# Head-mixing attention, routed experts and a dense layer in one kernel: scores and weighted sums move behind the transposing product of a slot

## The chip, the cores and the metric

The kernel runs on one core of one Trainium2 chip. The metric is the device time of one execution in microseconds (us), taken as the median of the runs shown. Engines are named as in the profile: PE is TensorE (PEld its weight loads), DVE is VectorE, ACT is ScalarE, POOL is GpSimd, SP is the engine whose queue starts most of the DMA transfers.

## The reference, cut to what matters

Three layers follow one another. The change touches the first one, attention with two mixes over the heads (4 batches, 12 heads, 448 positions, 64 values per head, all float32):

```python
scores = scale * np.matmul(q, k.transpose(0, 1, 3, 2))
scores = np.einsum('bhij,hg->bgij', scores, w_pre)
scores = scores - np.max(scores, axis=-1, keepdims=True)
attn = np.exp(scores)
attn = attn / (np.sum(attn, axis=-1, keepdims=True) + 1e-09)
attn = np.einsum('bhij,hg->bgij', attn, w_post)
return np.matmul(attn, v).astype(np.float32)
```

Its output feeds a layer of 8 routed experts, and that one a dense layer `g = h - tanh(h)` between two matrix products.

## The kernel before, in words

**Tiles and blocks.** The 4 x 448 query rows are cut into 16 tiles T of 120, 120, 120 and 88 rows per batch. A tile is cut into blocks of 10 rows (the last of a batch into 8 of 10 and one of 8), 180 blocks in all. A block holds 10 rows x 12 heads = 120 partitions, so that a mix over the heads is one product with a 120 x 120 matrix.

**The slot loop (L1013 to L1045).** One slot is one turn of a loop over s, written out in the order in which each engine is to do its work; there is no other planner. Each engine works through its own instructions in that order, and waits where a buffer or an input is not there yet. In slot s the kernel issues:

- P(s) (`emit_P`, L363): the head mix of block s on PE, as 2 matmuls into a PSUM bank of tag "b" (2 buffers). DVE takes the row maximum `mx` (L371); ACT makes p = exp (L374) and its sum.
- `emit_W` (L378) of block s-1 on DVE: the reciprocal of that sum and `w` = the second mixing matrix scaled by it (L381, L382, L384). It stands behind `mx` of block s on DVE.
- T(s-2) (`emit_T`, `T_mm`, L390 to L407): the transposing product of block s-2 on PE, 8 matmuls that mix the heads again, divide by the sum and turn the block, into a bank of tag "c" (2 buffers). It reads p and w of block s-2. ACT copies it out into A (`emit_TE`, L411).
- Fills, at slots fixed by formulas (`posS2`, `posAV`, `at_e`, L860 to L923): `emit_S2` (L428) makes the scores of 4 heads, 12 matmuls (L324), the first pair of heads into the two banks of tag "a", the second pair into "d" and "e" (one buffer each); ACT copies out the first pair (`ssb`, L331), then the bank "d" (`ssb`, L328), DVE the bank "e" (`ssb`, L329). `emit_AV2` (L438, L424) makes the weighted sums of 4 heads of a finished tile, 32 matmuls into bank "d", copied out by ACT (`xT`, L426). `tr_q` and `tr_k` transpose inputs into bank "e", copied out by ACT (`qh` L304, `kh` L287) and DVE (`ql` L305, `kl` L288). `emit_X` (L449) uses "e" as well.
- Routing pieces (`emit_R`, L483): small products R and M that each take one of the two "c" banks, and DVE work on them.
- Converting a piece of a later layer's weights (`conv_do`, L111): three DVE instructions (`ct`, L115 to L117), three on POOL (`cm`, L118 to L120).

Copies out of `emit_S`/`emit_S2` are issued at once; those of the other fills are kept in a list and issued by `flush` at the start of the next slot, or earlier when their bank is wanted again (`flush("d")`, `flush("e")`). DMA: `relay_to` (L939) sends a block's rows of the scores to `sr`, 8 buffers, 7 slots ahead of the P that reads them.

**Which slots have what.** Counted from the formulas, 44 of the 180 slots have a scores fill and 44 a weighted-sums fill; six (35, 42, 80, 87, 125 and 132) have both, so 38 have scores alone and 38 weighted sums alone. In a slot with both, scores come first. R stands in slots 64, 109, 154 and 177, M two slots later. Slot 180 has weighted sums and T(178), and no P.

The order in a slot is set by these lines:

```python
            ex = emit_P(s) if s < NBK else lambda: None
            if 0 <= s - 1 < NBK:
                emit_W(s - 1)
            ...
            fill.sort(key=lambda x: x[0] not in (emit_S, emit_S2, emit_AV2))
            if fill and fill[0][0] in (emit_S, emit_S2, emit_AV2):
                run_fill(*fill.pop(0))
            ex()
            ...
            if on:
                emit_T(i)
                T_mm(i, 0, NJ)
                flush("d")
                emit_TE(i)
            for x in fill:
                run_fill(*x)
```

`ex()` issues the exp of the slot; behind it stands the DVE and POOL work of `conv_do`. So PE's order in a slot with one such fill is P, fill, T, and the exp stands behind the copies of the scores on ACT. In a slot with both it is P, scores, T, weighted sums.

Of the kernel before, what the change touches and what calls it, by code (L numbers as in the profile page):

```python
# [30 lines left out]
def body(ctx: ExitStack, tc, q, k, v, w_pre, w_post, emb, tau, w1, w2, win, wout, out):  # L31
# [93 lines left out]
    if True:  # L125
# [237 lines left out]
        def emit_P(i):  # L363
            n = 12 * blocks[i][2]
            t = sr.pop(i)
            pt = ps("b", f"P{i}")
            pe.matmul(pt[:n, :S], wpre[:n, :n], t[:n, :], start=True, stop=True)  # L367

            flush2()
            mx = a2.tile([120, 4], F32, tag="mx", name=f"mx{i}", bufs=5)  # L370
            dve.tensor_reduce(mx[:n, 0:1], pt[:n, :S], op=ALU.max, axis=AX.X, negate=True)  # L371
            p = a2.tile([120, S], F32, tag="p", name=f"p{i}", bufs=LAG + 1)
            pj[i] = (p, mx)
            return lambda: act.activation(p[:n, :], pt[:n, :S], AF.Exp, bias=mx[:n, 0:1], scale=1.0, accum_out=mx[:n, 1:2])  # L374
# [3 lines left out]
        def emit_W(i):  # L378
            n = 12 * blocks[i][2]
            p, mx = pj[i]  # L380
            dve.tensor_scalar_add(mx[:n, 2:3], mx[:n, 1:2], 1e-9)  # L381
            dve.reciprocal(mx[:n, 3:4], mx[:n, 2:3])  # L382
            w = a2.tile([120, 120], F32, tag="w", name=f"w{i}", bufs=3)
            dve.tensor_scalar_mul(w[:n, :], wpost[:n, :], mx[:n, 3:4])  # L384
            wj[i] = w
# [4 lines left out]
        def emit_T(i):  # L390
            T, r, m = blocks[i]
            n = 12 * m
            b, it = divmod(T, 4)
            if r == 0:
                A[T] = aA.tile([CP, NJ, H, 120], F32, tag="A", name=f"A{T}", bufs=2)
            p, mx = pj.pop(i)
            w = wj.pop(i)
            wv = w.rearrange("p (g i) -> p g i", i=10)[:n, :, :m]
            pt = ps("c", f"T{i}")
            pv = pt[:CP, :NJ * n].rearrange("p (c g i) -> p c g i", c=NJ, i=m)  # L400
            tev[i] = (pt, pv, p, w, wv, n, m)

        def T_mm(i, c0, c1):
            pt, pv, p, w, wv, n, m = tev[i]
            for c in range(c0, c1):
                pe.matmul(pt[:CP, c * n:(c + 1) * n] if m == 10 else pv[:, c], p[:n, c * CP:(c + 1) * CP], w[:n, :] if m == 10 else wv,  # L406
                          start=True, stop=True)  # L407

        def emit_TE(i):
            T, r, m = blocks[i]  # L410
            act.copy(A[T][:, :, :, 10 * r:10 * r + m], tev.pop(i)[1])  # L411
# [202 lines left out]
    with mctx:  # L614
# [324 lines left out]
        def relay_to(i):  # L939
            while nxt[0] <= min(i, NBK - 1) and blocks[nxt[0]][0] in sdone:  # L940
                emit_relay(nxt[0])
                nxt[0] += 1
# [4 lines left out]
        def flush(tag=None):  # L947
            keep = []
            while late:
                x = late.pop(0)  # L950
                if tag in (None, x[0]):
                    y = x[1]()
                    if x[0] == "e" and callable(y):
                        late2.append((x[0], y))
                else:
                    keep.append(x)
            late.extend(keep)
            if tag:
                flush2(tag)
# [9 lines left out]
        def run_fill(fn, a):  # L969
            tag = "d" if fn is emit_AV2 else "e"  # L970
            if fn is emit_S2:
                flush("d")
                flush("e")
            elif fn is not emit_S:
                flush(tag)
            e = fn(*a)
            if fn in (emit_S, emit_S2):
                e()
                if a[1] + (fn is emit_S2) == NP - 1:
                    sdone.add(a[0])  # L980
            else:
                late.append((tag, e))
# [30 lines left out]
        for s in range(NBK + LAG + 6):  # L1013
            todo = side.get(s, [])
            fill = [x for x in todo if x[0] in PEF]
            for fn, a in todo:
                if fn in (load_q, load_k, load_v, conv_load, zero_fill):
                    fn(*a)
            flush()
            relay_to(s + NSR - 1)  # L1020
# [3 lines that stand above are left out]
            for fn, a in todo:  # L1024
                if fn is emit_R and a[1] in (0, 1, 3):
                    fn(*a)
            i = s - LAG
            on = 0 <= i < NBK
            fill.sort(key=lambda x: x[0] not in (emit_S, emit_S2, emit_AV2))
            if fill and fill[0][0] in (emit_S, emit_S2, emit_AV2):  # L1030
                run_fill(*fill.pop(0))
            ex()
            for fn, a in todo:
                if fn is conv_do:
                    fn(*a)
# [7 lines that stand above are left out]
            for fn, a in todo:  # L1043
                if fn in (to_experts, do1) or fn is emit_R and a[1] in (2, 4):
                    fn(*a)  # L1045
# [334 lines left out]
```

## Time and profile before

| | before |
|---|---|
| median of 3 runs | 1370.86 us (1370.37 to 1372.72) |
| the profiled execution | 1376.32 us, its span 1374.6 us |
| mean granted clock of PE | 0.977 of full speed |
| PE busy | 1312.8 us, 96% of the span |
| DVE busy | 1017.7 us, 74% |
| ACT busy | 736.7 us, 54% |
| POOL busy | 502.8 us, 37% |

The slot loop fills the span from about 24 us to 516 us; the experts and the dense layer follow. Busy times are unions per engine; a matmul's own duration overlaps its neighbour's, so that start-to-start distances tell what one costs PE.

### The profile page before, as it was taken

How to read it: one execution, taken by the hardware profiler on the slowest of the kernel's cores; microseconds unless marked ns; L12 is line 12 of the kernel's file. 1: busy time of each engine (PE TensorE's matmuls, PEld its weight loads, DVE VectorE, ACT ScalarE, POOL GpSimd, SP SyncE). 2: the span in 40 equal slices, each digit the busy share in tenths (PEclk: the TensorE clock that was granted, in tenths of full speed). 3: DMA queues.
4: the chain of work that ended last, by engine and by line, in shares of the span. 5: the costliest groups of instructions: out<-in, count | busy, mean ns of one | idle time of the engine just before them, and what ended most of it. 6: DMA issues, size and time to landing. Idle time of an engine off the chain costs nothing. (4 is left out here: it accounts for less than half of the span.)

```text
span 1374.6 us, 24956 instructions
## 1 busy us (share of the span) xinstructions
PE 1312.8 (96%) x9104; PEld 1146.0 (83%) x9104; DVE 1017.7 (74%) x2189; ACT 736.7 (54%) x1518; POOL 502.8 (37%) x495
## 2 busy tenths in 40 slices
PE   7999999999999987999999997899999989999998
PEld 5777776776777766999999996699998889999998
DVE  4776787678677773677776764688888788788886
ACT  5666666675666653545444453554444444544441
POOL 0233333333333323333332422544454334444432
PEclk9999999999999997999999999799999999999999
DMA  6886675667556564778877872421113133121102
GB/s 153 247 253 190 185 209 168 170 201 202 160 173 204 164 205 147 263 253 262 273 233 238 254 220 84 136 69 47 46 48 109 37 96 107 67 61 55 47 24 81
DMA packets 149412, 210.90 MB, mean 153 GB/s; under 512 B 54022, under 2 KB 109494, under 8 KB 149286
## 3 DMA queue, kind: packets, MB, share of 16 engines
q1 hardware_dynamic: 145104, 194.19, 46.4%
q0 software_dynamic: 2640, 12.19, 2.8%
q10 hardware_dynamic: 1542, 2.89, 0.7%
q8 instruction: 73, 1.20, 0.4%
q14 instruction: 53, 0.43, 0.1%
HBM read 135.70 MB, written 35.00 MB: 124 GB/s over the span
## 5 line engine op out<-in xcount | busy, mean ns | idle before, releaser
L406 PEld LDWEIGHTS T<-w,p 120*112 120x112 f32 (+1 forms) x1440 | 166.4, 177 | 66.8 <-issue 44.5
L120 POOL TENSOR_TENSOR cm<-cm,ct 128x256 f32<-128x256 f32 x96 | 70.1, 731 | 404.9 <-DVE ct L117 360.9
L406 PE MATMUL T<-w,p 120*112 120x120 f32 (+1 forms) x1440 | 185.6, 272 | 6.2 <-DVE w L384 3.0
L374 ACT ACTIVATE p<-P,mx 120x448 f32<-120x448 f32 x180 | 114.0, 633 | 119.8 <-DVE mx L381 106.3
L1220 POOL TENSOR_TENSOR gl<-th,gh 128x448 fp32r<-128x448 f32 x64 | 74.8, 1169 | 261.0 <-ACT gh L1219 192.6
L367 PE MATMUL P<-sr,wpre 120*120 120x448 f32 x360 | 166.2, 544 | 1.4 <-ACT p L374 1.4
L1271 PE MATMUL o<-woh,gh 128*128 128x384 f32 x448 | 152.5, 340 | 5.3 <-DVE acc L1277 5.3
L1240 ACT ACTIVATE u<-h 128x448 f32<-128x448 f32 x64 | 34.9, 546 | 222.9 <-PE h L1236 219.2
L1272 PE MATMUL o<-wol,gh 128*128 128x384 f32 x448 | 150.7, 336 | 0.0
L1273 PE MATMUL o<-woh,gl 128*128 128x384 f32 x448 | 150.7, 336 | 0.0
L371 DVE TENSOR_REDUCE mx<-P 120x1 f32<-120x448 f32 x180 | 111.4, 619 | 49.4 <-PE P L367 48.6
L1236 PE MATMUL h<-yh,wil 128*128 128x448 f32 x384 | 143.8, 374 | 3.3 <-POOL wil L1209 3.3
L1234 PE MATMUL h<-yh,wih 128*128 128x448 f32 x384 | 144.0, 375 | 1.1 <-ACT wih L1208 0.6
L1277 DVE TENSOR_TENSOR acc<-acc,o 128x384 f32<-128x384 f32 x196 | 106.9, 548 | 51.4 <-PE o L1273 51.4
L1235 PE MATMUL h<-yl,wih 128*128 128x448 f32 x384 | 143.9, 375 | 0.5 <-DVE yl L1183 0.5
L411 ACT COPY A<-T 112x480 f32<-112x480 f32 x180 | 101.5, 564 | 16.2 <-PE T L406 15.6
L686 PE MATMUL hi<-xhi,w1hi 128*128 128x256 f32 x384 | 108.8, 283 | 0.0
L687 PE MATMUL hi<-xli,w1hi 128*128 128x256 f32 x384 | 108.6, 283 | 0.0
L688 PE MATMUL hi<-xhi,w1li 128*128 128x256 f32 x384 | 108.4, 282 | 0.0
L424 PEld LDWEIGHTS AV<-A,v 112*64 112x64 f32 x1536 | 74.8, 138 | 23.9 <-issue 10.5
L669 PE MATMUL ypi<-w2hi,hhi 128*128 128x384 f32 x272 | 93.2, 343 | 0.1
L670 PE MATMUL ypi<-w2li,hhi 128*128 128x384 f32 x272 | 92.1, 338 | 0.6 <-DVE w2li L639 0.3
(223 smaller groups left out, 3279.9 us busy)
## 6 DMA issues: line engine op xcount, KB each, us to landing
sr<-ssb SPq DMA_DIRECT2D x176, 210.0 KB
r<-in_moe_w SPq DMA_DIRECT2D x72, 384.0 KB
r<-in_moe_w SPq DMA_DIRECT2D x52, 512.0 KB
craw<-in_moe_w_in SPq DMA_DIRECT2D x48, 256.0 KB
craw<-in_moe_w_out SPq DMA_DIRECT2D x48, 256.0 KB
raw<-wi_d SPq DMA_DIRECT2D x15, 768.0 KB
wor<-wo_d SPq DMA_DIRECT2D x15, 768.0 KB
wi_d<-cm SPq DMA_DIRECT2D x48, 128.0 KB
```

The costliest lines, as they stand in the source:

```text
L367: pe.matmul(pt[:n, :S], wpre[:n, :n], t[:n, :], start=True, stop=True)
L371: dve.tensor_reduce(mx[:n, 0:1], pt[:n, :S], op=ALU.max, axis=AX.X, negate=True)
L374: return lambda: act.activation(p[:n, :], pt[:n, :S], AF.Exp, bias=mx[:n, 0:1], scale=1.0, accum_out=mx[:n, 1:2])
L406: pe.matmul(pt[:CP, c * n:(c + 1) * n] if m == 10 else pv[:, c], p[:n, c * CP:(c + 1) * CP], w[:n, :] if m == 10 else wv, start=True, stop ...
L686: pe.matmul(pt[:, :256], wh[:, sl], xh[:, c, :], start=c == 0, stop=False)
L687: pe.matmul(pt[:, :256], wh[:, sl], xl[:, c, :], start=False, stop=False)
L1234: pe.matmul(pt[:, :S], wi[0][:, c, sl], yh[:, c, :], start=c == 0, stop=False)
L1235: pe.matmul(pt[:, :S], wi[0][:, c, sl], yl[:, c, :], start=False, stop=False)
L1236: pe.matmul(pt[:, :S], wi[1][:, c, sl], yh[:, c, :], start=False, stop=c == KD - 1)
L1271: pe.matmul(pt[:, :384], gh[:, sl], wo[0][:, f, n0:n0 + 384], start=f == 0, stop=False)
L1272: pe.matmul(pt[:, :384], gh[:, sl], wo[1][:, f, n0:n0 + 384], start=False, stop=False)
L1273: pe.matmul(pt[:, :384], gl[:, sl], wo[0][:, f, n0:n0 + 384], start=False, stop=f == GF - 1)
```

## The change

The two lines that run the first scores or weighted-sums fill ahead of `ex()` are gone. The fill stays in the list, at its head, and is run by the loop behind `emit_TE`. In a slot with one such fill PE's order becomes P, T, fill; in a slot with both it becomes P, T, scores, weighted sums. On ACT the exp and the copy of T come ahead of the copies of the scores; on DVE `conv_do` comes ahead of the copy of bank "e". No instruction is added or taken away.

```diff
             i = s - LAG
             on = 0 <= i < NBK
             fill.sort(key=lambda x: x[0] not in (emit_S, emit_S2, emit_AV2))
-            if fill and fill[0][0] in (emit_S, emit_S2, emit_AV2):
-                run_fill(*fill.pop(0))
             ex()
             for fn, a in todo:
                 if fn is conv_do:
```

## Rows read from the trace of the kernel before

**Rows 1.** Busy time by engine in the slot loop; columns: stretch, us, PE, PEld, DVE, ACT, POOL, clock, DMA.

```profile
24.00:510.00 486.00, 477.04 (x4092) 352.54 (x4092) 357.53 (x1114) 322.21 (x769) 160.71 (x219) 1.00 0.67 197
```

**Rows 2.** PE in order of time, slot 71, no such fill; columns: start, us, instruction.

```profile
211.28 0.92 PE L367 MATMUL P<-sr,wpre 120*120 120x448 f32 x2
212.03 0.98 PE L406 MATMUL T<-w,p 120*112 120x120 f32 x8
212.85 0.55 PE L281 MATMUL ptk<-ident,natk 112*128 112x112 f32 x4
```

**Rows 3.** PE in order of time, slot 42, which has both fills, and the next P.

```profile
132.26 0.46 PE L324 MATMUL S<-kh,qh 64*120 64x448 f32 x2
...
133.67 1.07 PE L406 MATMUL T<-w,p 120*112 120x120 f32 x8
134.72 1.86 PE L424 MATMUL AV<-A,v 112*64 112x120 f32 x32
136.51 1.01 PE L367 MATMUL P<-sr,wpre 120*120 120x448 f32 x2
```

**Rows 4.** DVE in order of time, slots 41 and 42: mx(41), w(40), mx(42).

```profile
131.60 0.61 DVE L371 TENSOR_REDUCE mx<-P 120x1 f32<-120x448 f32 x1
...
132.50 0.28 DVE L384 TENSOR_SCALAR w<-wpost,mx 120x120 f32<-120x120 f32 x1
132.70 0.62 DVE L371 TENSOR_REDUCE mx<-P 120x1 f32<-120x448 f32 x1
```

**Rows 5.** ACT in order of time, slots 41 and 42: copy of T, copies of the scores.

```profile
132.87 0.56 ACT L411 COPY A<-T 112x480 f32<-112x480 f32 x1
133.31 0.92 ACT L331 ACTIVATE ssb<-S 120x896 f32<-120x896 f32 x1
134.12 0.55 ACT L328 ACTIVATE ssb<-S 120x448 f32<-120x448 f32 x1
```

**Rows 6.** PE in order of time, slot 35: the scores' second pair of heads, the next P.

```profile
112.32 0.46 PE L324 MATMUL S<-kh,qh 64*120 64x448 f32 x1 [0.53 <-DVE kl L288]
...
115.90 1.01 PE L367 MATMUL P<-sr,wpre 120*120 120x448 f32 x2
```

**Rows 7.** DVE in order of time, slot 35: mx(35).

```profile
112.18 0.61 DVE L371 TENSOR_REDUCE mx<-P 120x1 f32<-120x448 f32 x1
```

**Rows 8.** All engines in order of time, slot 132: mx(132), and the next P.

```profile
387.77 0.62 DVE L371 TENSOR_REDUCE mx<-P 120x1 f32<-120x448 f32 x1
...
390.46 0.64 PE L367 MATMUL P<-sr,wpre 120*120 120x448 f32 x1
```

**Rows 9.** All engines in order of time, slots 9 and 174: P(s), w(s-2).

```profile
41.71 0.92 PE L367 MATMUL P<-sr,wpre 120*120 120x448 f32 x2
42.85 0.28 DVE L384 TENSOR_SCALAR w<-wpost,mx 120x120 f32<-120x120 f32 x1
...
494.05 0.92 PE L367 MATMUL P<-sr,wpre 120*120 120x448 f32 x2
494.87 0.28 DVE L384 TENSOR_SCALAR w<-wpost,mx 120x120 f32<-120x120 f32 x1
```

**Rows 10.** All engines in order of time, slots 64 and 154, which have R: weighted sums, A.

```profile
191.09 1.86 PE L424 MATMUL AV<-A,v 112*64 112x120 f32 x32
191.36 0.56 ACT L411 COPY A<-T 112x480 f32<-112x480 f32 x1
...
445.03 1.86 PE L424 MATMUL AV<-A,v 112*64 112x120 f32 x32
445.76 0.56 ACT L411 COPY A<-T 112x480 f32<-112x480 f32 x1
```

**Rows 11.** All engines in order of time, slot 180: weighted sums, w(178).

```profile
512.86 2.88 PE L424 MATMUL AV<-A,v 112*64 112x120 f32 x32
513.16 1.69 DVE L384 TENSOR_SCALAR w<-wpost,mx 120x120 f32<-120x120 f32 x1
```

**Rows 12.** Busy time by engine and granted clock, last slots of the loop; columns as in rows 1.

```profile
510.00:515.00 5.00, 3.12 (x36) 3.03 (x38) 4.86 (x9) 2.22 (x6) 4.01 (x2) 0.85 0.44 130
```

## The prediction

> **What bounds the kernel now.** I read the busy time of the stretch that the change touches first, then PE's order of time in three kinds of slot, and then DVE's and ACT's beside it. In the 486 us of the slot loop PE is busy for 477.04 us, at the full granted clock; DVE and ACT have 357.53 and 322.21 us [rows 1]. So PE sets the pace, 2.7 us a slot, with 9 us of pauses in all. The same matmuls run after the change, so PE's work stays; what can change is how long PE waits, and PE's next wait is what to look for. A slot without these fills costs PE 0.75 us for P (211.28 to 212.03) and 0.82 us for T [rows 2]. Scores take 1.41 us and weighted sums 1.79 us [rows 3]. Today these 1.4 or 1.8 us stand between P and T, and so they are a reserve: whatever T needs may come that much later than P's end and costs nothing. After the change the reserve is gone, and the fill has it: whatever the fill needs may come 0.8 us later than now.
>
> **The change part by part.** All terms are against the profiled execution (1376.32 us, which is 5.5 us over the median of the runs shown); I carry their sum over to the median.
>
> *A, slots with both fills (six).* Now T stands between scores and weighted sums on PE; after the change nothing does, and both use the one bank "d". The weighted sums can begin only when ACT has copied the scores out of it (`ssb`, L328), and that copy now stands behind the exp, the copy A of T and the other score copy. ACT's chain from the maximum on: mx starts at 131.60, A at 132.87, that is 1.27 us [rows 4, 5]; A to the first score copy 0.44 us, first to second copy 0.81 us, the second lasts 0.55 us [rows 5]; together 3.07 us from the start of mx(s) to a free bank. In slot 42 mx(42) starts at 132.70 [rows 4], so the bank is free at 135.77, the weighted sums end 1.79 us later at 137.56, and P follows there, now at 136.51 [rows 3]: 1.05 us lost. (T(40) waits for w(40), which ends at 132.78 [rows 4], half a microsecond after it could begin; this wait lies inside the 1.05.) Slot 87 shows the same times. In slot 35 mx starts at 112.18 [rows 7], the bank is free at 115.25, P follows at 117.04 instead of 115.90 [rows 6]: 1.14 us, and slots 80 and 125 repeat it. In slot 132 mx starts late, at 387.77: 390.84, then 392.63 instead of 390.46 [rows 8], 2.17 us. Sum 2 x 1.05 + 3 x 1.14 + 2.17 = 7.7 us. The lower end is an ACT that is free when the scores end, which leaves only its two copies there, worth nothing; the upper end, if ACT's instructions do not overlap (0.56 and 0.92 us instead of 0.44 and 0.81 [rows 5], and as much again for the exp), is 0.5 us more per slot, 10.7 us.
>
> *B, T waits for w in slots with one fill.* Behind a T that waits stand on PE the fill and the next P, and with them DVE's next mx. Where w(s-2) ends more than 0.75 us after P(s) starts, PE now waits in front of T. In slot 9 w ends at 43.13, and T could begin at 41.71 + 0.75 = 42.46: 0.67 us. In slot 174 it is 495.15 against 494.80, 0.35 us [rows 9]. There are four such slots; the two between them, 13 and 135, read in the same way, have 0.42 and 0.80 us. In each w is late for a cause in an earlier slot (DVE waits for a copy by ACT of a transpose or of X, or does a conversion), which the change does not move. Together 2.2 us. In five more slots w comes within 0.2 us of that point, and there the exp, now earlier on ACT, helps; I take 0.4 us for them, and 0 to 1.2 us as ends. Sum 2.6 us, ends 1 and 5.
>
> *C, R and M slots.* R takes one of the two "c" banks, so T needs the bank of the slot before, after A's copy. Now the weighted sums lie in front of T and hide that. After the change T could begin where the weighted sums begin now, at 191.09 in slot 64, but the copy A ends at 191.92; in slot 154 it is 446.32 against 445.03 [rows 10]. That is 0.83 and 1.29 us, and slot 109 between them, read in the same way, has 1.28 us: 3.4 us for the three of them. In the M slots two later the same holds for scores, partly used up by the first wait; following DVE's queue I take 1 us more there, for 4.4 us, with ends 2 and 7. Slot 177 costs nothing: its T waits for DVE past the weighted sums already today.
>
> *D, slot 180.* T(178) cannot begin before w ends at 514.85; today the weighted sums, from 512.86 on, fill that time [rows 11]. Behind T they come after it. PE's queue behind T holds the weighted sums, T(179) and the last X. The sums last 2.88 us here; some of this is made good since T(179) has its w by then. I take 1.0 us, ends 0 and 2.9.
>
> *E, what is won.* In six slots the second half of the scores waits for bank "e", which DVE frees with kl ([0.53 <-DVE kl], [rows 6]). T in front gives it 0.8 us, and the wait ends. Three of the six are slots with both fills, where term A has it inside. In the other three (25, 70, 115) up to 0.8 us each is free, but DVE and ACT come no earlier: in two of them the copy of "e", now behind a conversion, and the next w are late instead. I take 1.5 us won, ends 0 and 2.4.
>
> *What costs nothing.* The exp and A come earlier on ACT and the copies later; ACT has 164 us of idle time in the loop [rows 1], and outside the six slots nobody needs these copies within a slot. The copy of the weighted sums goes to the start of the next slot, in front of an exp that waits for mx anyhow; X reads it two slots later. If that cover went, it would be 0.4 us in each of 38 slots, 15 us. No fill issues a DMA, and SP's order stays; relays of a tile's last scores wait up to 1.5 us longer, six slots (16 us) ahead of the P that needs them. POOL gets its conversion data earlier.
>
> Sum: 7.7 + 2.6 + 4.4 + 1.0 - 1.5 = 14.2 us. 1370.9 + 14.2 = 1385.
>
> A T between scores and weighted sums takes 1.05 us, against 0.82 us elsewhere [rows 2, 3]: each change between full and split use of the array costs about 0.12 us. In slots with one fill there are two such changes in either order, so I count none. By the Trainium skill (TensorEngine Tiling (Array Packing), section Key Properties) switching the tiling mode drains the engine; the slots with both fills then go from four switches to three, 0.12 us less in six slots, and the sum would be 13.5 us.
>
> **The rivals.** *Faster, by the freed wait.* T in front of the scores takes away the wait for kl, and ACT's copies are early enough. It is decided at the L328 copy in slots 35, 80 and 125: it wins if bank "d" is free within 0.8 us of the end of the scores. Then the six waits go, each 0.8 to 1.0 us of start-to-start distance, about 5.5 us, and the time is 1365. For it speaks the 0.53 us row [rows 6]; against it that mx(35) itself stands behind kl on DVE [rows 7], and the chain of 3.07 us behind mx.
>
> *No change.* PE's pauses only move: what is lost in the slots is made good by the waits after it, since DVE and ACT catch up while PE stands. 1371. For it: late w and A mean that PE is ahead, and a wait makes later ones shorter. Against it: PE pauses only 9 us in the whole loop [rows 1], so there is little to give back.
>
> *Slower still, by the clock.* In the last slots PE is busy for only 3.12 of 5 us; the mean granted clock of that stretch is 0.85, part of it at 2.4 and part at 1.2 GHz [rows 12], and the weighted sums take 2.88 instead of 1.86 us [rows 3, 11]. If each of the six pauses of term A is followed by the lower level, 1.0 us more each time, the time is 1391. Against it: those pauses are single and stand in a busy stretch, and the loop with its 9 us of pauses keeps a clock of 1.00 [rows 1]. The Trainium skill (TensorE: Matmul & The Clock Gate, section Why this matters for your kernels) warns that pauses between bursts of matmuls bring the lower clock back; no row here shows it for a single pause within the loop.
>
> **How the numbers follow.** Forecast (1385, itself from 1377 to 1396) 0.70; faster by the freed wait 0.05; no change 0.06; the clock 0.15; 0.04 for something worse, waits that pass on from slot to slot. The lower ends sum to 0 + 1 + 2 + 0 - 2.4 = 0.6 us, the upper ones to 10.7 + 5 + 7 + 2.9 = 25.6 us, and the clock adds 6: 1371 to 1402. Not all ends come together; 1374 to 1400 leaves out the faster case, no change and a little at the top. A measurement of this kernel can tell about 0.2% (2.7 us) from no change. Faster 0.05, within 0.2% 0.06, slower 0.89.
>
> **What would show it.** In the new profile the stretch of the loop is about 14 us longer, with PE's busy time in it unchanged. In PE's order of time the weighted sums of slots 35, 42, 80, 87, 125 and 132 wait for ACT `ssb`, 1 to 2.5 us. T's group names DVE w and ACT A as releasers, with several us more than now, and scores no longer wait for kl. If the weighted sums in the six slots begin right behind the scores, term A is wrong; if T's idle time stays, B and C are; if the granted clock in the loop falls under 1.00, the third rival is at work.

## The result and the profile after

The changed kernel takes 1387.53 us (median of 4 runs, 1385.98 to 1389.47) against 1370.61 us before (also a median of 4): 1.0119 times as long, 95% interval 1.0102 to 1.0136, so 16.9 us slower. Its profiled execution took 1385.98 us, with a span of 1384.3 us and a mean granted clock of 0.978.

The first view is the one of [rows 1], now from the first to the last P of each kernel: before, then after (stretch, us, PE, PEld, DVE, ACT, POOL, clock, DMA).

```profile
23.92:508.72 484.80, 476.12 (x4088) 352.21 (x4087) 356.28 (x1111) 322.07 (x768) 160.02 (x218) 1.00 0.67 197
```

```profile
22.51:524.77 502.26, 479.69 (x4089) 363.27 (x4087) 352.36 (x1113) 321.95 (x768) 162.92 (x219) 0.99 0.66 191
```

The same work takes 17.5 us more. PE's pauses grow from 8.7 to 22.6 us, 13.9 us; PE's busy time grows by 3.6 us, and the clock is no longer 1.00. So most of the loss is waiting, and a fifth of it, by busy time, is slower matmuls. The groups of instructions by line say for what PE waits (last columns: idle time before the group, and what ended it); before, then after:

```profile
L406 PE MATMUL T<-w,p 120*112 120x120 f32 (+1 forms) x1440 | 185.6, 272 | 6.2 <-DVE w L384 3.0 <-DVE pos L520 1.6 <-ACT A L411 1.4
L424 PE MATMUL AV<-A,v 112*64 112x120 f32 (+1 forms) x1536 | 85.2, 264 | 0.0
L324 PE MATMUL S<-kh,qh 64*120 64x448 f32 (+1 forms) x192 | 44.1, 425 | 3.1 <-DVE kl L288 2.7 <-ACT ssb L331 0.4
```

```profile
L406 PE MATMUL T<-w,p 120*112 120x120 f32 (+1 forms) x1440 | 180.5, 269 | 12.5 <-DVE w L384 6.6 <-ACT A L411 4.5 <-DVE idr L538 1.4
L424 PE MATMUL AV<-A,v 112*64 112x120 f32 (+1 forms) x1536 | 87.4, 268 | 9.8 <-ACT ssb L328 9.8
L324 PE MATMUL S<-kh,qh 64*120 64x448 f32 (+1 forms) x192 | 40.6, 418 | 0.6 <-ACT ssb L331 0.4 <-ACT qh L304 0.2
```

A wait that was not there, of the weighted sums for the copy `ssb` of L328, has 9.8 us, all of it in the six slots with both fills; T's idle time has doubled, with 6.6 instead of 3.0 us for w and 4.5 instead of 1.4 us for A; and the scores' wait for kl is gone. Slot 42 after the change, PE and then ACT, to be read against [rows 3, 5]:

```profile
133.58 1.04 PE L406 MATMUL T<-w,p 120*112 120x120 f32 x8 [0.59 <-DVE w L384]
134.56 0.47 PE L324 MATMUL S<-kh,qh 64*120 64x448 f32 x2
...
136.87 1.86 PE L424 MATMUL AV<-A,v 112*64 112x120 f32 x32 [0.83 <-ACT ssb L328]
138.66 1.01 PE L367 MATMUL P<-sr,wpre 120*120 120x448 f32 x2
```

```profile
134.00 0.64 ACT L374 ACTIVATE p<-P,mx 120x448 f32<-120x448 f32 x1
134.54 0.19 ACT L374 ACTIVATION_READ_ACCUMULATOR p<-P,mx 120x1 f32 x1
134.66 0.58 ACT L411 COPY A<-T 112x480 f32<-112x480 f32 x1
135.47 0.92 ACT L331 ACTIVATE ssb<-S 120x896 f32<-120x896 f32 x1 [0.23 <-PE S L324]
136.28 0.54 ACT L328 ACTIVATE ssb<-S 120x448 f32<-120x448 f32 x1
```

Both waits of the prediction stand in one slot: 0.59 us in front of T, for w, and 0.83 us in front of the weighted sums, which begin 0.05 us after the copy of bank "d" has ended (136.28 + 0.54 = 136.82). On ACT the exp and the copy A now come first. In slot 35 the exp is later, because mx stands behind kl, and the wait is longer; PE, and then ACT's exp and its copy of bank "d":

```profile
112.11 0.47 PE L324 MATMUL S<-kh,ql 64*120 64x448 f32 x2
114.77 1.86 PE L424 MATMUL AV<-A,v 112*64 112x120 f32 x32 [2.18 <-ACT ssb L328]
116.56 1.01 PE L367 MATMUL P<-sr,wpre 120*120 120x448 f32 x2
```

```profile
112.29 0.63 ACT L374 ACTIVATE p<-P,mx 120x448 f32<-120x448 f32 x1 [1.28 <-DVE mx L381]
...
114.16 0.55 ACT L328 ACTIVATE ssb<-S 120x448 f32<-120x448 f32 x1
```

From P to P, the slots compare like this (start-to-start distances of P in the two traces, differences summed over the slots named):

| slots | before to after, us |
|---|---|
| 35, 42, 80, 87, 125, 132 (both fills) | +1.25, +1.49, +2.78, +1.51, +1.26, +2.24: +10.5 |
| 9, 13, 135, 174 (late w) | +0.80, +0.75, +0.68, +0.48: +2.7 |
| 64 to 67, 109 to 112, 154 to 157 (R and M) | +2.7 |
| 175 to 178 (R in 177) | +3.2 |
| 25 to 28, 70 to 73, 115 to 118 (scores waited for kl) | -1.9 |
| the other 141 slots | +0.3 |

Their sum is 17.5 us. At the last X of attention 15.7 us are left, mostly since a stretch at the lower clock that the kernel before had there now falls into slot 177. In the experts, which the change does not touch, the profiled executions differ by 5 us the other way (334.8 us before and 330.1 us after, from the last X to the dense layer's first transpose). The ten traces of this case have 328.6 to 334.8 us there, whatever was changed in the slot loop; the kernel before has the longest, which fits its profiled execution, 1376.32 us, standing above its own median.

### The profile page after: what moved, and what is told of

Same layout as the page of the kernel before. It is cut to its first block, busy times and chain, and to the rows that moved or that the text cites. A ratio compares the mean times of both kernels' runs of the same rounds, so it can differ in the third digit from the quotient of the medians.

```text
span 1384.3 us, 24960 instructions
## 1 busy us (share of the span) xinstructions
PE 1311.8 (95%) x9104; PEld 1152.8 (83%) x9104; DVE 1012.5 (73%) x2189; ACT 736.9 (53%) x1518; POOL 501.9 (36%) x495
## 5 line engine op out<-in xcount | busy, mean ns | idle before, releaser
L406 PEld LDWEIGHTS T<-w,p 120*112 120x112 f32 (+1 forms) x1440 | 170.6, 178 | 88.0 <-issue 56.5
L406 PE MATMUL T<-w,p 120*112 120x120 f32 (+1 forms) x1440 | 180.5, 269 | 12.5 <-DVE w L384 6.6
L367 PE MATMUL P<-sr,wpre 120*120 120x448 f32 x360 | 171.4, 558 | 1.4 <-ACT p L374 1.4
L424 PE MATMUL AV<-A,v 112*64 112x120 f32 (+1 forms) x1536 | 87.4, 268 | 9.8 <-ACT ssb L328 9.8
L119 POOL TENSOR_SCALAR cm<-cm 128x256 f32<-128x256 f32 x96 | 88.9, 926 | 8.4
```

## The experiments

My theory was that of the prediction: a fill in front of T hides what T waits for, and T in front of a fill puts ACT's exp and A ahead of the copies that free bank "d". The rivals were that pauses only move, or that DVE and ACT set the pace whatever PE's order. Ratios are to the kernel before, run on the same chip beside them; its median is 1372.07 us beside the first four runs below and 1369.76 us beside the last four, so a loss in us is taken against the median beside the run.

**The six slots back in the old order.** Edit against the changed kernel:

```diff
             fill.sort(key=lambda x: x[0] not in (emit_S, emit_S2, emit_AV2))
+            if s in (35, 42, 80, 87, 125, 132):
+                run_fill(*fill.pop(0))
             ex()
```

> The changed kernel, but in the six slots with both fills (35, 42, 80, 87, 125, 132) the scores run ahead of the exp and of T again. Theory (the weighted sums wait for bank d behind ACT's chain exp, A, two score copies): the 10.5 us that these six slots lost come back, and the waits of slots 9, 13, 64, 109, 135, 154, 174 and 177 stay: about 1377 us, 1.005 of the kernel before; no PE wait for ssb. Rival (pauses only move; PE that is earlier there waits elsewhere): 1384 us or more.

Measured: 1379.47 us, 1.0045 (1.0029 to 1.0061). The six slots are back to 0.01 us of the kernel before in sum, the weighted sums wait for nothing (0.0 us of idle time in their group), and the slots with late w, R and M keep most of their losses (7.7 of 8.5 us). So rather more than half of the loss sits in six of 180 slots (9.5 of 16.9 us by the times, the loss now being 7.4 us; 10.5 of 17.5 us by the trace), and a pause taken away there does not come back elsewhere.

**The six slots alone in the new order.** Edit against the kernel before:

```diff
-            if fill and fill[0][0] in (emit_S, emit_S2, emit_AV2):
+            if fill and fill[0][0] in (emit_S, emit_S2, emit_AV2) and s not in (35, 42, 80, 87, 125, 132):
                 run_fill(*fill.pop(0))
             ex()
```

> The kernel before, with the new order in the six slots with both fills alone. Theory: it loses 9 to 11 us in these six slots and nothing elsewhere, about 1380.5 us, 1.007 of the kernel before; six PE waits for ssb L328 of 0.8 to 2.2 us. Rival (the loss needs the whole schedule): within 2 us of the kernel before.

Measured: 1384.67 us, 1.0095 (1.0072 to 1.0118), more than expected. The six waits are those of the changed kernel, 9.8 us. But here, after the pause of 2.19 us in slot 35, the matmuls behind it are slow too. PE in order of time, slots 35 and 36, and then the mean clock of a stretch of them:

```profile
115.11 2.12 PE L424 MATMUL AV<-A,v 112*64 112x120 f32 x32 [2.19 <-ACT ssb L328]
117.16 1.85 PE L367 MATMUL P<-sr,wpre 120*120 120x448 f32 x2
118.80 1.57 PE L406 MATMUL T<-w,p 120*112 120x120 f32 x8
120.20 0.86 PE L458 MATMUL X<-ien,xT 128*120 128x136 f32 x6
```

```profile
116.60:120.00 3.40, 3.40 (x17) 2.23 (x14) 0.89 (x4) 0.60 (x2) 0.01 (x1) 0.50 0.90 181
```

P takes 1.64 us and T 1.40 us from start to start, where [rows 2] have 0.75 and 0.82 us: the clock is at 1.2 GHz. The same happens after slots 80 and 125. Slots 36 and 126 lose 1.4 and 1.3 us by it, and slot 80 1.3 us more than slots 35 and 125 do in the changed kernel; with smaller pieces the loop loses 14.0 us, 5.0 us more than the 9.0 us that the six slots lose at the full clock (as in the changed kernel, with 1.25 us in slot 80 as in slots 35 and 125).

**Late w, R and M slots and slot 180 in the old order.** Edit against the changed kernel:

```diff
+            if s in (9, 13, 64, 66, 109, 111, 135, 154, 156, 174, 177, 180):
+                run_fill(*fill.pop(0))
             ex()
```

> The changed kernel, but in slots 9, 13, 135, 174 (late w), 64, 66, 109, 111, 154, 156, 177 (R and M) and 180 the fill runs ahead of T again. Theory (a fill in front of T hid w and A there): the 2.7 us of the four slots, some 2.7 us of the R and M slots and 3 us at slot 177 come back, 1379 us, 1.006 of the kernel before; T's waits for w and A are left only in slots 42, 87 and 132. Rival (DVE sets the pace there, so PE's order does not matter): 1386 us or more.

Measured: 1382.56 us, 1.0064 (1.0042 to 1.0086). Slots 9, 13, 135, 174 and 177 are back to the kernel before within 0.1 us, 64, 109 and 154 too; T's idle time falls from 12.5 to 8.3 us, of which ACT A has 1.5. The mechanism holds, and the ratio is the one expected. In us, the loss comes down by 6.4 us by the times (from 16.9 to 10.5) and by 6.5 us in the loop by the trace, instead of 8.5: this execution has the lower clock after slot 35 (1.3 us in slot 36) that the changed kernel's had not, and the runs scatter (1378 to 1385 us).

**The new order only where w is in time.** Edit against the kernel before:

```diff
-            if fill and fill[0][0] in (emit_S, emit_S2, emit_AV2):
+            if fill and fill[0][0] in (emit_S, emit_S2, emit_AV2) and not (
+                    fill[0][0] is emit_S2 and s not in (9, 13, 35, 42, 54, 66, 80, 87, 99, 111, 125, 132, 144, 156)):
                 run_fill(*fill.pop(0))
             ex()
```

> The kernel before, with the new order only in the 30-odd slots that have scores alone and in which w is in time (not 9, 13, 54, 66, 99, 111, 144, 156). Theory: the waits of the scores for bank e in slots 25, 70 and 115 go (1.9 us) and shorter ones in slots like 29, 58, 74, 103 and 119 (0.15 to 0.24 us each, 1.7 us), with nothing lost: 1367 us, 0.997 of the kernel before. Rival (DVE and ACT set the pace, so a wait of PE that goes comes back at the next T): 1370.5 us, no change; if a copy of bank e late by a conversion costs more, 1372 us.

Measured: 1371.68 us, 0.9995 (0.9981 to 1.0008), no change, which is the time of the rival. The waits for kl do go (slots 25, 70 and 115 are 0.85, 0.80 and 0.91 us shorter). In 26 and 71 0.42 and 0.48 us come back, where tk waits for bank "e" (1.09 us from T to tk in slot 26, instead of 0.82); and in slots 39, 84 and 129, weighted sums in the old order right behind scores in the new one, 0.43 us each:

```profile
122.15 1.01 PE L367 MATMUL P<-sr,wpre 120*120 120x448 f32 x2
123.42 1.86 PE L424 MATMUL AV<-A,v 112*64 112x120 f32 x32 [0.26 <-ACT ssb L328]
```

This is slot 39: weighted sums come 1.27 us after P instead of 0.85, because the copy of bank "d" of the slot before is late. In sum the loop is 1.0 us shorter, and the measurement cannot tell that from nothing. So most of the gain does come back, but at the banks "e" and "d" that exist once, and not, as the rival had it, at the next T.

**The exp behind the scores' copies.** Edit against the changed kernel, in the six slots:

```diff
-            ex()
+            if s not in (35, 42, 80, 87, 125, 132):
+                ex()
...
-            for x in fill:
+            for n_, x in enumerate(fill):
                 run_fill(*x)
+                if s in (35, 42, 80, 87, 125, 132) and n_ == 0:
+                    ex()
```

> The changed kernel, but in the six slots with both fills the exp stands behind the scores' copies on ACT instead of ahead of T's copy; PE's order is that of the changed kernel. Theory (bank d comes free 3.07 us after mx because exp and A stand in front of the copies): the weighted sums wait about 0.9 us behind the scores in all six slots instead of 0.8 to 2.2 us; slots 35, 80 and 125 come back to about 6.0 us, 42, 87 and 132 stay 1.3 us over the kernel before; 7 us of 10.5 come back: 1380.5 us, 1.007 of the kernel before. Rival (the two copies themselves and the switch of the array are the price, whatever stands before them): 1386 us or more.

Measured: 1380.65 us, 1.0072 (1.0051 to 1.0092), as the theory had it. PE's order is that of the changed kernel, and only ACT's is changed. PE, slot 35:

```profile
112.21 0.47 PE L324 MATMUL S<-kh,ql 64*120 64x448 f32 x2
113.41 1.86 PE L424 MATMUL AV<-A,v 112*64 112x120 f32 x32 [0.73 <-ACT ssb L328]
115.20 1.01 PE L367 MATMUL P<-sr,wpre 120*120 120x448 f32 x2
```

The wait of 2.18 us is down to 0.73 us, the two copies themselves; slots 35, 80 and 125 are 0.2 us shorter than before, 42, 87 and 132 1.50 us longer. The six slots lose 3.9 us instead of 10.5; 1.5 us of the difference is the lower clock of slot 80, which does not show here.

**Bank "d" copied first.** Edit against the changed kernel (cur[0] holds s):

```diff
-                e0()
-                e1()
+                (e1 if cur[0] in (35, 42, 80, 87, 125, 132) else e0)()
+                (e0 if cur[0] in (35, 42, 80, 87, 125, 132) else e1)()
```

> The changed kernel, but in the six slots with both fills ACT copies bank d before the two banks a. Theory: bank d comes free 0.81 us earlier where ACT is behind (35, 80, 125, 132) and 0.1 to 0.2 us earlier in 42 and 87, where the scores themselves end late: 3.6 us less, and the lower clock in slot 80 goes with its shorter pause: 1383 us, 1.009 of the kernel before. Rival (another bank or engine holds the weighted sums): no change, 1387 us.

Measured: 1382.98 us, 1.0101 (1.0078 to 1.0124). In slot 35 the wait is 1.38 us, 0.80 us less than 2.18; the six slots lose 5.3 us instead of 10.5, of which 1.5 us is the lower clock of slot 80 that does not show here. The times alone do not tell this kernel from the changed one, whose 1.0119 lies within the interval; the waits do. Both runs together say that it is ACT's order, instruction by instruction, that sets when the weighted sums begin.

**Weighted sums first in the six slots.** Edit against the kernel before, so that PE's order there is P, weighted sums, T, scores:

```diff
-            fill.sort(key=lambda x: x[0] not in (emit_S, emit_S2, emit_AV2))
+            fill.sort(key=lambda x: (x[0] not in (emit_S, emit_S2, emit_AV2), x[0] is not emit_AV2))
```

> The kernel before, but in the six slots with both fills the weighted sums run ahead of T and the scores behind it: P, weighted sums, T, scores. Theory: bank d is copied out (0.36 us) while T runs, so nobody waits for it, and the scores no longer wait for kl in slots 35, 80 and 125 (0.9 us each): 1368 us, 0.998 of the kernel before. Rival (as in the picked slots, what PE wins there comes back as a wait at the next T or tk): 1370.5 us, no change.

Measured: 1368.54 us, 0.9987 (0.9974 to 1.0000), at the edge of what can be told. The trace shows what was expected: slots 35, 80 and 125 are 1.0 us shorter each, the loop 3.1 us, and nothing comes back. PE, slot 35:

```profile
108.47 0.92 PE L367 MATMUL P<-sr,wpre 120*120 120x448 f32 x2
109.32 1.86 PE L424 MATMUL AV<-A,v 112*64 112x120 f32 x32
111.11 1.07 PE L406 MATMUL T<-w,p 120*112 120x120 f32 x8
112.12 0.46 PE L324 MATMUL S<-kh,qh 64*120 64x448 f32 x2
...
113.52 1.01 PE L367 MATMUL P<-sr,wpre 120*120 120x448 f32 x2
```

5.05 us from P to P without a pause, against 6.04 before and 7.3 after the change.

**The same, with T ahead of the scores in three more slots (111, 115 and 119).** Edit against the kernel with the weighted sums first:

```diff
-            if fill and fill[0][0] in (emit_S, emit_S2, emit_AV2):
+            if fill and fill[0][0] in (emit_S, emit_S2, emit_AV2) and s not in (111, 115, 119):
                 run_fill(*fill.pop(0))
```

> As the kernel with the weighted sums first, and in addition slots 111, 115 and 119 have T ahead of the scores. Theory: another 0.9 us at slot 115, 0.6 at 111 and 0.2 at 119, which the run with picked slots kept (its gain there did not come back): 1366.5 us, 0.997 of the kernel before. Rival: 1370.5 us, no change.

Measured: 1369.23 us, 0.9990 (0.9969 to 1.0010), no change. Slots 115 and 119 give 0.92 and 0.24 us as expected; slot 111, an M slot, loses 3.0 us. Its choice was a mistake: it had the old order in the run with picked slots, so the 0.6 us it won there was not the new order's, and its T has to wait for A as in term C, here for 1.94 us; the lower clock follows that pause as well.

## Why the prediction was right, point by point

It said 1385 us, between 1374 and 1400, and 1387.5 came out; the likeliest case was the one that happened. That the sum came so near is in part luck. Against the trace (15.7 us to the last X), A and slot 177 were 2.8 and 3.2 us too low, and C, D and E 1.7, 2.7 and 0.4 us too high, which nearly cancels. And 4.5 us of the loss, 1.5 in slot 80 and 3.0 in slot 177, are a lower clock that the sum did not hold: PE's busy time in the loop, which was to stay, grew by 3.6 us.

**A (7.7 us, measured 10.5).** Mechanism and place were right, slot by slot: in slots 42, 35 and 132 P moved by 1.49, 1.25 and 2.24 us where the working had 1.05, 1.14 and 2.17. The part missing is that the chain behind mx was taken over from the old order, in which the scores are there before ACT comes to copy them: in slot 42 it is now 0.81 us from A to the first score copy (134.66 to 135.47) instead of 0.44, as A and the copy no longer overlap and ACT waits 0.23 us for the first scores, and the weighted sums begin 0.05 us after the end of the last copy. Slot 80 has 2.78 us instead of 1.25, and that is the third rival, below; at the full clock the six slots lose 9.0 us. The lower end, an ACT with only its two copies to do, was "worth nothing"; the run with the exp behind shows that case, and it costs 3.9 us, as slots 42, 87 and 132 still wait, 0.6 us for w and 0.85 us for the copies. The runs with the exp behind and with bank "d" first show that ACT's order is the cause, the run with the old order in the six slots that the term stands by itself.

**B (2.6 us, measured 2.7).** The four slots lose 0.80, 0.75, 0.68 and 0.48 us for 0.67, 0.42, 0.80 and 0.35.

**C (4.4 us, measured 2.7).** Slots 64, 109 and 154 lose 1.0, 1.3 and 1.3 us, as worked out (0.83, 1.28 and 1.29). The 1 us added for the M slots was wrong in sign: slots 66 and 156 lose 0.4 us, but 111 and the slots behind (67, 112, 157) get 0.2 to 0.6 us back each. In 67 and 112 these are T's waits for A of the kernel before (0.40 and 0.47 us), which are gone, with the copy A now earlier on ACT. Here pauses did move.

**"Slot 177 costs nothing" (measured 3.2 us).** As a forecast of the time this step failed, but by the clock and not by the order. T does begin when w is there, as today. PE now stands still until then, where it ran weighted sums before, and in this execution what comes behind the pause runs at the lower clock. PE in order of time, and the clock:

```profile
517.36 1.91 PE L406 MATMUL T<-w,p 120*112 120x120 f32 x8 [2.60 <-DVE w L384]
519.20 3.47 PE L424 MATMUL AV<-A,v 112*64 112x120 f32 x32
522.60 1.51 PE L367 MATMUL P<-sr,wpre 120*120 120x448 f32 x2
523.95 0.98 PE L406 MATMUL T<-w,p 120*112 120x120 f32 x8
```

```profile
517.00:524.00 7.00, 6.64 (x43) 5.53 (x44) 5.02 (x13) 1.66 (x4) 4.21 (x3) 0.53 0.76 254
```

T takes 1.84, the weighted sums 3.40 and P 1.35 us, against 0.82, 1.79 and 0.75 us [rows 2, 3]. In the run with the exp behind, slot 177 has the same order and the same pause, and the matmuls behind it keep the full clock:

```profile
511.36 1.05 PE L406 MATMUL T<-w,p 120*112 120x120 f32 x8 [2.60 <-DVE w L384]
512.34 1.86 PE L424 MATMUL AV<-A,v 112*64 112x120 f32 x32
514.13 1.01 PE L367 MATMUL P<-sr,wpre 120*120 120x448 f32 x2
514.98 0.98 PE L406 MATMUL T<-w,p 120*112 120x120 f32 x8
```

There slot 177 loses 1.86 us and slot 178, whose T no longer waits, gets 1.77 us back: slots 175 to 178 lose 0.2 us in all. So the order alone costs next to nothing, as the prediction had it, and 3.0 of the 3.2 us are the lower clock.

**D (1.0 us, measured -1.7 from the last P to the last X).** Wrong in sign, mostly for the same reason: before, the lower clock came after the pauses in front of slot 180; now it has come earlier, and the last slots run at the full clock. With the old order and the full clock there (the run with the weighted sums first) these last slots take 15.3 us instead of the 16.5 us before, so 1.2 of the 1.7 us are the clock. For the rest, DVE caught up during the slow stretch, and T waits 0.34 and 1.44 us there instead of 2.16 us for w alone. With the exp behind, where slot 177 kept the full clock, T waits 2.07 us twice, the lower clock follows, and the last slots take 19.6 us, 3.1 us more than before: the cost that D looked for depends on what slot 177 does.

**E (1.5 us won, measured 1.9).** The wait for kl went; in 26 and 71 a part came back, as said. Not foreseen: the 30 other slots with scores alone are 2.0 us shorter in sum, mostly through short waits for banks (0.13 to 0.24 us in nine of them), and the slots behind them and the others longer by nearly as much. That the number of changes between full and split array stays fits the +0.3 us of these 141 slots.

**The rivals.** Faster by the freed wait: the wait went, but bank "d" came free 2.2 us too late in slots 35, 80 and 125, which was the point that decides. No change: without the six slots, the run with the new order only where w is in time came out at that time, though what came back there came back at the banks "e" and "d". The clock: it came true in part. One of the six pauses (slot 80) and the pause in 177 were followed by the lower level in the profiled execution, three of the six where they alone had the new order. It was given 0.15 as a case of its own, all or nothing; it is rather a surcharge that some executions pay.

## What to carry to other kernels

Before a filler is moved, ask what it hides at its old place and what it will wait for at its new one; both can be read from the trace before, as the distance between the end of the late operand and the point where the moved instruction would begin. Two users of a buffer that exists once need something between them on the critical engine, and the copy that frees the buffer should not stand behind other work in its own queue; which of the two goes first is then worth trying, as here, where the weighted sums first wait for nothing. A loss that is found in a handful of the iterations should be sought there, by listing start-to-start distances of one instruction in both traces.

## What the runs showed of the hardware

A single pause of PE within a busy stretch can bring the lower clock, and need not. In the changed kernel slots 35, 80 and 125 have the same pause, of 2.18 to 2.19 us; after slots 35 and 125 the matmuls run on at full clock (in slot 35 the weighted sums take 1.86 us, above), after slot 80 they do not:

```profile
243.96 3.40 PE L424 MATMUL AV<-A,v 112*64 112x120 f32 x32 [2.18 <-ACT ssb L328]
247.29 1.01 PE L367 MATMUL P<-sr,wpre 120*120 120x448 f32 x2
```

```profile
243.60:247.20 3.60, 3.24 (x32) 3.09 (x32) 0.00 (x0) 0.31 (x1) 0.00 (x0) 0.53 0.90 201
```

The mean granted clock there is 0.53, the 1.2 GHz level for nearly all of it, and the weighted sums cost 1.5 us more. With the six slots alone in the new order it happened after all three pauses of 2.19 us. The pause of 2.60 us in slot 177 was followed by the lower level in three of the four traces that have it, and not in the one shown above. What decides it, these runs do not show. A pause of about 2 us thus costs itself and, in some executions, 1.3 to 1.5 us behind it in the slots with both fills.
